# Two spectral layers on one Trainium2 core: the time transform taken ahead of the feature transform

## The chip, the cores and the metric

The kernel runs on one core of one Trainium2 chip. The time is that of the device in microseconds, from the start of the program to its end; lower is better. The engines are TensorE (PE, with its weight loads as PEld), VectorE (DVE), ScalarE (ACT), GpSimd (POOL) and SyncE (SP, which only issues DMAs).

## What is computed

The input x has 2048 time steps (rows) of 512 features. Two layers follow each other, each a spectral part and a feed-forward part:

```python
x = x + irfft2(rfft2(layernorm(x)) * (w_r + 1j * w_i))     # over time and features, 257 feature frequencies
n = layernorm(x)
x = x + ((n @ w_gate) * (n @ w_up)) @ w_down               # 512 -> 1792 -> 512
# both lines a second time, with the same weights
```

All is float32. The feed-forward part takes most of the time and is the same in both kernels; the change is in the spectral part.

## The kernel before, in words

**Layout.** The rows lie as 16 row tiles t of 128: time step 32p + 2t + jj stands on partition (jj, p), with p up to 63 and jj 0 or 1. `xs` holds x in SBUF all along.

**Spectral part, forward** (`fwd`, `fwd_rest`, L562 to L626), once per row tile: statistics of the layer norm and the reciprocal deviation (`stats`, `rstd`, tiles st, mv, rs); `fo`, sums and differences of the two halves of the features (additions on DVE, differences on POOL); `tp`, four turns of 128x128 on PE that bring the features to the partitions; `fb` and `fs`, a copy and a second fold of the features; `dp`, four 128x128 products with the cosine and sine matrices `df`, which end the feature transform; `us`, a copy that multiplies with the reciprocal deviation; `sp`, the part of the time transform that runs over p, with twiddles, as products over 64 partitions each (two at a time on the two halves of the array's rows) and 257 columns; copies of sp into `E`. Eight row tiles of layer 1 are turned through memory in place of tp (`by_memory`).

**Middle** (`middle`, L650 to L729), for 16 blocks of 16 feature frequencies: DVE turns 32x32 blocks of E into `T` (`turn`), `zp` multiplies with the 32-point transform `f2` over the 32 values of (t, jj), two ACT copies make `jz` (i times zp), DVE and POOL multiply with the filter (`wq`, `wr`), DVE adds into `ys` (in five blocks a second product with g2j adds on PE), `yp` transforms back, ACT copies into T, and DVE turns back into E. Frequency 256 goes apart (`tx`, `xp`, `hp`).

**Inverse** (`inv`, L731 to L778), per row tile: `vp`, the time part over p, four 128x128 products; a copy `vs`; `yi`, the inverse feature products (with 256 columns in "plain" tiles, 128 in "fold" tiles); additions of yi into xs; statistics for the next norm. vp of the first half of the frequencies waits for the first eight blocks only.

**Feed-forward part** (`unit`, `down` and others): products gx, gy, gw, gz, gv, db, ex to ev of three passes each. Six plain row tiles and two fold tiles of the inverse come before it or at its start; eight more tiles of the inverse lie inside its first half, and in layer 0 half of the next layer's `fwd` lies inside its second half.

**What sets the order.** The kernel's functions don't issue instructions; they record operations in a `Plan` (L175) with an engine, an estimated cost, the tiles read and written, and at some places a due time. `Plan.order` works the due times backwards, `run` lays the operations out by due time, and 250 moves from a list of seeds (`MOVES`) change due times again. Each engine then works its list strictly in order. All recorded operations are issued by one line of a helper, so nearly all rows of the profile say L417; tiles tell them apart. Buffers come in rings (`RINGS`): f (ten working tiles of 128x512), tw for the twiddles, and the eight PSUM banks x, y, w (one each), a (three), d (two).

The rates that the plan assumes for PE:

```python
pe(0.98, features, [(fs, 0), (fs, 1), df], [dp])             # forward, per row tile
pe(0.1 + 0.97 * (b - a) / 257, times, [u, tw], banks)         # sp
pe(0.86 * len(ms), unspec, [y, (q, 0), (q, 1)], [yp])         # middle, per block
pe(0.82 if fold else 1.73, features, [vs, di], [yi])          # inverse
```

## Time and profile before

| | |
|---|---|
| median of 3 runs | 1086.56 us |
| lowest and highest | 1084.35 and 1087.3 us |
| span of the profiled execution | 1082.8 us |
| granted TensorE clock | 1.000 |
| HBM read and written | 151.85 and 49.02 MB |

The profiled execution has no other time than its span, from the first to the last instruction; the runs' median lies 3.8 us above it. How to read it: the page gives busy times of the engines over the span; the views of the trace give the same by stretches of time (us, then busy us and number of instructions of PE, PEld, DVE, ACT, POOL, then the granted clock, the DMA share and GB/s), by groups of equal instructions, and as a timeline. A count in a row is of records: a product of plain float32 operands is two records, a turn or a product of the feed-forward part one.

### The profile page before, as it was taken

How to read it: one execution, taken by the hardware profiler on the slowest of the kernel's cores; microseconds unless marked ns; L12 is line 12 of the kernel's file. 1: busy time of each engine (PE TensorE's matmuls, PEld its weight loads, DVE VectorE, ACT ScalarE, POOL GpSimd, SP SyncE). 2: the span in 40 equal slices, each digit the busy share in tenths (PEclk: the TensorE clock that was granted, in tenths of full speed). 3: DMA queues.
4: the chain of work that ended last, by engine and by line, in shares of the span. 5: the costliest groups of instructions: out<-in, count | busy, mean ns of one | idle time of the engine just before them, and what ended most of it. 6: DMA issues, size and time to landing. Idle time of an engine off the chain costs nothing.

```text
span 1082.8 us, 18693 instructions
## 1 busy us (share of the span) xinstructions
PE 1062.9 (98%) x6404; PEld 913.4 (84%) x6404; DVE 839.6 (78%) x1660; ACT 445.7 (41%) x1021; POOL 766.5 (71%) x988
## 2 busy tenths in 40 slices
PE   8999999999999999999999999999999999999998
PEld 6748988888889988888997489888889998888887
DVE  8597877877868866676787978679897877667777
ACT  6777743443343223222346776124332521222330
POOL 7377798989999766658784627466597984676771
PEclk9999999999999999999999999999999999999999
DMA  7545357787771766575564313665877257546542
GB/s 270 219 156 195 117 202 252 232 273 226 255 262 51 235 233 202 158 226 181 144 205 160 125 61 104 204 198 165 222 251 211 70 199 248 173 167 198 192 145 78
DMA packets 104446, 202.08 MB, mean 187 GB/s; under 512 B 56352, under 2 KB 70176, under 8 KB 93344
## 3 DMA queue, kind: packets, MB, share of 16 engines
q0 software_dynamic: 16128, 102.77, 29.2%
q1 hardware_dynamic: 87936, 97.60, 27.6%
q8 instruction: 51, 0.84, 0.3%
q10 hardware_dynamic: 288, 0.52, 0.1%
q14 instruction: 43, 0.35, 0.1%
HBM read 151.85 MB, written 49.02 MB: 186 GB/s over the span
## 4 chain that ended last, share of the span: by engine, by line
PE 80%; POOL 6%; DVE 6%; ACT 2%; DMA 2%; issue 2%; SPq 0%; DVEq 0%; POOLq 0%; ACTq 0%
PE gz L417 13%; PE gx L417 12%; PE gv L417 7%; PE db L417 6%; PE gy L417 6%; PE gw L417 6%; PE ex L417 5%; PE ez L417 5%; PE yi L417 3%; PE ey L417 3%; PE sp L417 2%; PE ev L417 2%; PE ew L417 2%; PE dp L417 2%; PE vp L417 2%
## 5 line engine op out<-in xcount | busy, mean ns | idle before, releaser
L417 PE MATMUL gx<-xA,wt 128*128 128x512 f32 (+1 forms) x852 | 180.8, 347 | 2.9 <-ACT xA L417 1.1
L417 PEld LDWEIGHTS gx<-xA,wt 128*128 128x128 f32 x852 | 137.1, 189 | 21.3 <-DVE xA L417 1.4
L417 POOL TENSOR_TENSOR sf<-q,sf 128x256 fp32r<-128x256 f32 x101 | 75.1, 744 | 39.6 <-ACT sf L417 35.8
L417 DVE TENSOR_TENSOR xs<-xs,db 128x512 f32<-128x512 f32 x128 | 85.6, 683 | 14.8 <-PE db L417 14.5
L417 DVE TENSOR_TENSOR q<-gy,s 128x512 f32<-128x512 f32 (+1 forms) x71 | 41.0, 578 | 64.2 <-PE gy L417 46.5
L417 PE MATMUL gw<-xS,wt 128*128 128x512 f32 (+1 forms) x426 | 90.3, 347 | 0.3 <-POOL wt L417 0.3
L417 PE MATMUL gz<-xS,wt 128*128 128x512 f32 (+1 forms) x426 | 90.0, 347 | 0.1
L417 PE MATMUL gz<-xA,wt 128*128 128x512 f32 (+1 forms) x426 | 90.0, 347 | 0.0
L417 PE MATMUL gv<-xS,wt 128*128 128x512 f32 (+1 forms) x426 | 89.9, 346 | 0.0
L417 PE MATMUL gy<-xS,wt 128*128 128x512 f32 (+1 forms) x426 | 89.6, 346 | 0.0
L417 PE MATMUL db<-wd,h 128*128 128x512 f32 x336 | 89.1, 393 | 0.3
L417 ACT CAST sf<-q 128x256 fp32r<-128x256 f32 x101 | 41.1, 407 | 116.0 <-DVE q L417 71.8
L417 POOL TENSOR_TENSOR sf<-cc,sf 128x256 fp32r<-128x256 f32 x96 | 71.4, 745 | 19.1 <-ACT sf L417 18.7
L417 POOL DMA_DIRECT2D wt<-gu x72 | 40.5, 562 | 62.7 <-PE gz L417 42.9
L417 PEld LDWEIGHTS gz<-xA,wt 128*128 128x128 f32 x426 | 69.5, 189 | 10.1 <-DVE q L417 0.3
L417 PEld LDWEIGHTS gz<-xS,wt 128*128 128x128 f32 x426 | 68.6, 190 | 9.4 <-DVE q L417 0.7
L417 PEld LDWEIGHTS gw<-xS,wt 128*128 128x128 f32 x426 | 68.6, 190 | 9.0 <-POOL wt L417 0.5
L417 PEld LDWEIGHTS gv<-xS,wt 128*128 128x128 f32 x426 | 68.6, 190 | 8.9 <-issue 0.3
L417 PEld LDWEIGHTS gy<-xS,wt 128*128 128x128 f32 x426 | 68.5, 190 | 8.4
L417 ACT COPY s<-gx 128x512 f32<-128x512 f32 (+1 forms) x71 | 35.3, 496 | 87.6 <-PE gx L417 77.1
L417 PEld LDWEIGHTS db<-wd,h 128*128 128x128 f32 x336 | 60.7, 188 | 11.9 <-DVE xs L417 0.7
L417 POOL TENSOR_TENSOR wt<-rg,wt 128x512 fp32r<-128x512 f32 (+1 forms) x56 | 64.2, 1158 | 6.6 <-ACT wt L417 6.6
(171 smaller groups left out, 2644.2 us busy)
## 6 DMA issues: line engine op xcount, KB each, us to landing
wt<-gu POOLq DMA_DIRECT2D x36, 1024.0 KB, 5.5
wt<-gu POOLq DMA_DIRECT2D x36, 768.0 KB, 4.8
bf<-dn POOLq DMA_DIRECT2D x20, 1024.0 KB, 5.4
bf<-dn POOLq DMA_DIRECT2D x20, 768.0 KB, 4.7
gu<-wt SPq DMA_DIRECT2D x14, 1024.0 KB, 6.6
gu<-wt SPq DMA_DIRECT2D x14, 768.0 KB, 3.6
wq<-in_wf_dram SPq DMA_DIRECT2D x10, 1024.0 KB, 5.1
rg<-in_wb_dram SPq DMA_DIRECT2D x14, 512.0 KB, 5.0
```

Source lines behind the costliest of these rows:

```text
L417: ins = f(*args, **kw)
```

## The change

**Forward.** The time part over p comes first, straight on the rows: `tp` is now four products of fo (as stationary operand) with the twiddle matrix `tw`, 128 columns each. That brings the features to the partitions too, so the turns by PE and through memory, fb, us and sp go. The reciprocal deviation is multiplied into tw by ACT. Rows are real, so of 64 time residues 32 are kept; E holds features on the partitions, and 4 blocks, 16 row tiles, 16 pairs g and 8 values along the columns. In layer 0 the twiddles come in four loads.

**Middle.** 16 groups g, each a pair of time residues. Second feature fold `fs` (one half on POOL, one on DVE); `dp`, eight products with a stationary operand of 64 columns, whose results go to the lower and the upper 64 partitions in turn; a copy `zs`; `zp`, the 32-point transform; jz, filter and addition as before, always on DVE and POOL; `vq`, four 128x128 products that transform back and bring the frequencies to the partitions; a copy into E in runs of four elements. No 32x32 turns on E. Frequency 256 shares a column with frequency 0; a small DVE operation (8 columns) per filter load prepares that.

**Inverse.** yi first, straight from E, a copy or a fold into vs, then `yo`, one product of 512 columns, for the time part. yi needs all 16 groups.

**Filter.** Eight loads of 1 MB go to the buffers xA, xS and wd of the feed-forward part.

**rstd.** A pair of row tiles shares its small DVE operations (128x2 in place of two of 128x1).

**Order.** The moves are replaced by a list of due times, one for each operation (`DUES`). Rings: f 11 for 10, tw 8 for 4. The instructions of the feed-forward products keep their numbers; their order is another.

The core of the diff (constants, tables and the parts that follow from these are left out):

```diff
-    RINGS = {"x": 1, "y": 1, "w": 1, "a": 3, "d": 2, "f": 10, "tw": 4, "mv": 8, "rs": 8, "st": 2,
+    RINGS = {"x": 1, "y": 1, "w": 1, "a": 3, "d": 2, "f": 11, "tw": 8, "mv": 8, "rs": 8, "st": 2,
...
+        found = np.frombuffer(zlib.decompress(base64.b85decode("".join(DUES))), "<i2")
+        assert len(found) == len(ops)
+        for o, due in zip(ops, found):
+            o["due"] = int(due) * 0.1
+        return self.run()
...
-        ts = V.tensor_scalar
-        for i in range(n):
-            c = lambda j, i=i: v()[:, j, i:i + 1]
-            m = lambda j, i=i: mv()[:, i, j:j + 1]
-            dve(10, lambda c=c, m=m: ts(c(1), m(1), EPS, c(1), op0=ALU.add, op1=ALU.mult), [(mv, i)], [(v, 1, i)])
-            dve(10, lambda c=c: ts(c(2), c(1), -1.5, c(0), op0=ALU.add, op1=ALU.mult), [(v, 0), (v, 1, i)], [(v, 2, i)])
-            if not fwd:
-                dve(10, lambda c=c, m=m: ts(c(3), m(0), -1.0, c(2), op0=ALU.mult, op1=ALU.mult), [(v, 2, i), (mv, i)],
-                    [(v, 3, i)])
+        c = lambda j: v()[:, j, :n]
+        m = lambda j: mv()[:, :n, j]
+        vs = lambda j: [(v, j, i) for i in range(n)]
+        dve(10, lambda: stt(c(1), m(1), EPS, c(1), op0=ALU.add, op1=ALU.mult), mvs, vs(1))
+        dve(10, lambda: stt(c(2), c(1), -1.5, c(0), op0=ALU.add, op1=ALU.mult), [(v, 0), *vs(1)], vs(2))
+        if not fwd:
+            dve(10, lambda: stt(c(3), m(0), -1.0, c(2), op0=ALU.mult, op1=ALU.mult), [*vs(2), *mvs], vs(3))
...
-        tw = twiddle(tf, t)
+        tw = tws[t] if tws else twiddle(tf, t)
+        act(128, lambda: A.mul(tw(), tw(), nm.v()[:, 2, i:i + 1]), [(nm.v, 2, i)], [tw], more=0.1)
         fo = temp("fo", "f", (128, 4, 128))
         x0, x1 = (xs[:, t, 256 * h:256 * h + 256].rearrange("p (a d) -> p a d", a=2) for h in range(2))
         pool(256, lambda: gtt(fo()[:, 2:4], x0, x1, ALU.subtract), [("xs", t)], [(fo, 1)])
-        dve(256, lambda: tt(fo()[:, 0:2], x0, x1, ALU.add), [("xs", t)], [(fo, 0)], two=True)
-        fs, fb = temp("fs", "f", (128, 4, 128)), temp("fb", "f", (128, 4, 128))
-        if mem:
-            by_memory(lambda: fo().rearrange("p a d -> p (a d)"), f"f{t}", lambda: fb().rearrange("p a d -> p (a d)"), [fb],
-                      None, [(fo, 0), (fo, 1)])
+        if on_pool:
+            pool(256, lambda: gtt(fo()[:, 0:2], x0, x1, ALU.add), [("xs", t)], [(fo, 0)])
         else:
-            tp = bank("tp", tags(t)[0])
-
-            def turn():
-                for j in range(4):
-                    TE.transpose(tp()[:, 128 * j:128 * j + 128], fo()[:, j], ident)
-
-            pe(0.44, turn, [(fo, 0), (fo, 1), "ident"], [tp])
-        quarter = lambda v, j: v().rearrange("p (a j) d -> p a j d", j=2)[:, :, j]
-        ta, tb = (lambda j=j: tp().rearrange("p (a j d) -> p a j d", a=2, j=2)[:, :, j] for j in range(2))
-        if mem:
-            pool(256, lambda: gtt(fs()[:, 2:4], quarter(fb, 0), quarter(fb, 1), ALU.subtract), [fb], [(fs, 1)])
-            pool(256, lambda: gtt(fs()[:, 0:2], quarter(fb, 0), quarter(fb, 1), ALU.add), [fb], [(fs, 0)])
-        elif on_pool:
-            act(512, lambda: A.copy(fb(), tp().rearrange("p (j d) -> p j d", j=4)), [tp], [fb])
-            pool(256, lambda: gtt(fs()[:, 2:4], quarter(fb, 0), quarter(fb, 1), ALU.subtract), [fb], [(fs, 1)])
-        else:
-            act(256, lambda: A.copy(quarter(fb, 1), tb()), [tp], [fb])
-            dve(256, lambda: tt(fs()[:, 2:4], ta(), quarter(fb, 1), ALU.subtract), [tp, fb], [(fs, 1)])
-        if not mem:
-            dve(256, lambda: tt(fs()[:, 0:2], ta(), quarter(fb, 1), ALU.add), [tp, fb], [(fs, 0)])
-        dp = bank("dp", tags(t)[1])
+            dve(256, lambda: tt(fo()[:, 0:2], x0, x1, ALU.add), [("xs", t)], [(fo, 0)], two=True)
+        tp = bank("tp", tag(t))
+
+        def spread():
+            for b in range(4):
+                TE.matmul(tp()[:, 128 * b:128 * b + 128], fo()[:, b], tw(), start=True, stop=True, skip_group_check=True)
+
+        pe(0.9, spread, [(fo, 0), (fo, 1), tw], [tp])
+        act(512, lambda: A.copy(E()[:, :, t].rearrange("p b g e -> p b (g e)"), tp().rearrange("p (b c) -> p b c", b=4)), [tp], [(E, t)], due=due)
...
+        def load(self, n):
+            load(1024, lambda: SP.dma_start(self.part(n), wf[:, n]), (), [self.key[n]], ahead=FAHEAD)
+            dve(8, lambda: stt(self.part(n)[:, :, :, 0], self.part(n)[:, :, :, 0], 0.5, hp[:, :, 4 * n:4 * n + 4],
+                               op0=ALU.mult, op1=ALU.add), ["hp"], [self.key[n]])
...
-            pe(0.1 + 0.97 * (b - a) / 257, times, [u, tw], banks)
...
-            pe(0.86, lambda z=z, n=n: TE.matmul(z(), f2, T()[:, 16 * n:16 * n + 16], start=True, stop=True), [(T, n), "midt"], [zp])
...
+        fs = temp("fs", "f", (128, 4, 16, 8))
+        folds = FOLDS[g % len(FOLDS)]
+        for i, op in ((0, ALU.add), (1, ALU.subtract)):
+            args = [*es], [(fs, i), (E, "g", g, i)]
+            if folds[i] == "P":
+                pool(256, lambda i=i, op=op: gtt(fs()[:, 2 * i:2 * i + 2], src(0), src(1), op), *args)
+            else:
+                dve(256, lambda i=i, op=op: tt(fs()[:, 2 * i:2 * i + 2], src(0), src(1), op), *args, two=True)
+        dp = bank("dp", "xy"[g % 2] if g < 13 else "x")
...
+            f4 = fs().rearrange("p j t (e q) -> p j (t e) q", q=2)
+            for q in range(2):
+                for j, c, odd in ((0, 0, 0), (2, 1, 0), (3, 0, 1), (1, 1, 1)):
+                    o = 256 * q + 128 * odd
+                    TE.matmul(dp()[64 * c:64 * c + 64, o:o + 128], f4[:, j, :, q], df()[:, j], start=True, stop=True,
+                              skip_group_check=True)
...
+        zs = temp("zs", "f")
+        act(512, lambda: A.copy(zs(), dp()), [dp], [zs])
+        zp = bank("zp", "da"[g % 2])
+
+        def across():
+            if g:
+                TE.matmul(zp(), f2, zs(), start=True, stop=True)
             else:
+                for q, m in enumerate((f20, f2)):
+                    TE.matmul(zp()[:, 256 * q:256 * q + 256], m, zs()[:, 256 * q:256 * q + 256], start=True, stop=True, skip_group_check=True)
+
+        pe(0.86, across, [zs, "midt"], [zp])
+        jz, y = temp("jz", "f"), temp("ys", "f")
+        act(512, lambda: A.mul(jz()[0:64], zp()[64:128], -1.0), [zp], [(jz, 0)], more=0.11)
+        act(512, lambda: A.copy(jz()[64:128], zp()[0:64]), [zp], [(jz, 1)], more=0.11)
+        w = W.key[g // 2]
+        dve(512, lambda: tt(zp(), zp(), W(g, 0), ALU.mult), [(jz, 0), (jz, 1), w], [zp])
+        pool(512, lambda: gtt(jz(), jz(), W(g, 1), ALU.mult), [w], [(jz, 0), (jz, 1)])
+        dve(512, lambda: tt(y(), zp(), jz(), ALU.add), [zp, (jz, 0), (jz, 1)], [y])
+        vq = bank("vq", "w" if g < 13 else "yw"[g % 2])
+
+        def back():
+            for q in range(2):
+                for par in range(2):
+                    o = 256 * q + 128 * par
+                    TE.matmul(vq()[:, o:o + 128], y()[:, o:o + 128], g2 if g or q else g20, start=True, stop=True, skip_group_check=True)
+
+        pe(0.92, back, [y, "midt"], [vq])
+        into = lambda: E()[:, :, :, g].rearrange("p b t (q e) -> p q (b t) e", q=2)
+        act(512, lambda: A.copy(into(), vq().rearrange("p (q c e) -> p q c e", q=2, e=4)), [vq], [(E, "g", g, 0), (E, "g", g, 1)], due=due)
...
-            pe(0.46, lambda par=par: times(par), [tw, *((E, "b", n) for n in range(8 * par, 8 * par + 8))], [(vp, par)], due=early)
...
-        act(512, lambda: A.copy(vs(), vp()), vps, [vs])
...
+                TE.matmul(yi()[:, o], E()[:, i, t], di()[:, i, 0:128 if fold else 256],
...
+        pe(0.9 if fold else 1.73, features, [*((E, "g", g, 0) for g in range(16)), di], [yi], due=early)
...
+            act(512, lambda: A.copy(vs(), yi()), [yi], [(vs, 0), (vs, 1)])
...
+        pe(0.88, lambda: TE.matmul(yo(), tw(), vs(), start=True, stop=True), [tw, (vs, 0), (vs, 1)], [yo])
```

More of the change, by code (lines that the diff above doesn't have):

```diff
@@ new lines, in consts @@
+    f[0, 1] = g[0, 1] = (1.0 - 2.0 * (p % 2))[:, None]
+    tf = np.zeros((2, 64, 16, 16, 2, 2, 2))
+    ti = np.zeros((64, 2, 16, 2, 64))
+    for jj in range(2):
+        tf[jj, :, :, :, :, jj] = f.reshape(16, 2, 2, 64, 16, 2)[..., jj].transpose(3, 4, 0, 2, 1)
+        ti[:, jj, :, jj] = g.reshape(64, 64, 16, 2)[..., jj].transpose(0, 2, 1)
+    w = np.exp(-2j * np.pi * (np.outer(j, j) % 32) / 32)
+    late = np.exp(-1j * np.pi * j / 32)[:, None] * w
+    unit = np.array([1.0, 1j])
+    fs, gs = [], []
@@ L311, in run @@
         for o in ops:
-            if not o["n"] and not o["out"]:
+            if not o["n"]:
                 enter(o)
@@ L346, in run @@
             first = min(a for a, _ in nexts)
-            if first > mark + 20.0:
-                mark = first
-                marks.append((len(out), first, {g: list(q) for g, q in rings.items()}, dict(free), bus, port, dict(after)))
             at, o = min((c for c in nexts if c[0] <= first + look), key=lambda c: (c[1]["due"], c[1]["i"]))
-            if o["e"] == "PE":
-                assert not pace or at < pace[done]
-                done += 1
             ready[o["e"]].remove(o)
@@ L1178 @@
             begins.append(t)
[L1179 to L1181 removed]
+            u = UNITS[layer][k >= 18]
+            t += (UFIRST if k < 2 else u[0]) if half is not None else u[1] if k < 12 else u[2]
             if k == 1:
```

489 lines of the change are left out of this document (196 added, 293 removed), and 35 rows, old and new, of the table MOVES.

## The prediction

> **What bounds the kernel now.** I read the page first, then busy time by stretches, then TensorE's timeline at the stage borders, then the groups of instructions. (In all rows: PE is TensorE, PEld its weight loads; a timeline row is start, duration, instructions; a group row ends in busy time, mean ns of one, and idle time before.)
>
> ```profile
> span 1082.8 us, 18693 instructions
> PE 1062.9 (98%) x6404; PEld 913.4 (84%) x6404; DVE 839.6 (78%) x1660; ACT 445.7 (41%) x1021; POOL 766.5 (71%) x988
> ```
> ```profile
> 70.00:80.00 10.00, 10.00 (x28) 4.74 (x27) 10.00 (x18) 8.64 (x16) 9.64 (x10) 1.00 0.20 60
> 700.00:800.00 100.00, 100.00 (x598) 88.91 (x598) 86.43 (x164) 34.56 (x79) 64.71 (x94) 1.00 0.67 201
> ```
> PE is busy 98% of the span and all of 700 to 800 us, a stretch of the feed-forward part. So PE work that is saved inside that part is saved time, and a new order of it can hardly win more. In the middle of a spectral stage (70 to 80) PE and DVE are both full, and POOL nearly. The spectral stages stand between these rows:
>
> ```profile
> 49.21 1.98 PE L417 MATMUL zp<-T,midt 128*128 128x512 f32 x4 [0.63 <-DVE T L417]
> 85.96 1.70 PE L417 MATMUL vp<-tw,E 128*128 128x128 f32 x12 [1.01 <-DVE E L417]
> 109.22 0.86 PE L417 MATMUL gx<-xA,wt 128*128 128x256 f32 x5 [0.34 <-DVE xA L417]
> ...
> 588.60 4.56 PE L417 MATMUL zp<-T,midt 128*128 128x512 f32 x10 [0.63 <-DVE T L417]
> 623.88 1.70 PE L417 MATMUL vp<-tw,E 128*128 128x128 f32 x12 [1.01 <-DVE E L417]
> ```
> The forward part of layer 0 ends at 49.2; the middles last 36.8 us (49.21 to 85.96) and 35.3 us (588.60 to 623.88); the feed-forward part begins near 109.
>
> **What one piece of PE work costs.** A record's duration holds its drain, so I use distances from start to start.
>
> ```profile
> 30.65 0.60 PE L417 MATMUL tp<-ident,fo 128*128 128x128 f32 x4
> 31.08 1.06 PE L417 MATMUL dp<-df,fs 128*128 128x128 f32 x8
> ...
> 37.69 2.00 PE L417 MATMUL sp<-us,tw 64*128 64x257 f32 x16
> 39.62 0.55 PE L417 MATMUL tp<-ident,fo 128*128 128x128 f32 x3
> ```
> ```profile
> 582.00 2.94 PE L417 MATMUL dp<-df,fs 128*128 128x128 f32 x24
> 584.87 3.10 PE L417 MATMUL sp<-us,tw 64*128 64x257 f32 x32
> ```
> ```profile
> 615.29 1.02 PE L417 MATMUL zp<-T,midt 128*128 128x512 f32 x2
> 616.14 1.02 PE L417 MATMUL yp<-ys,midt 128*128 128x512 f32 x2
> ```
> ```profile
> 97.25 1.10 PE L417 MATMUL vp<-tw,E 128*128 128x128 f32 x8
> 98.19 1.06 PE L417 MATMUL yi<-di,vs 128*128 128x128 f32 x8
> ```
> Four turns tp: 0.43 us. Four 128x128 products (dp): 2.87/3 = 0.957. One row tile's time transform sp: 1.93/2 = 0.965. One 512-column product: 0.855. One vp: 0.94.
>
> **Layer 0, forward.** PE's work per row tile falls from tp + dp + sp to one spread tp of four 128x128 products: 0.957 (same shape as dp). PE is then no longer the limit; DVE is, which has statistics, additions and the small rs operations to do.
>
> ```profile
> 4.48 0.69 DVE L417 BATCH_NORM_STATS2 st<-xs 128x6 f32<-128x512 f32 x1 [3.60 <-DMA xs<-in_x_dram]
> ...
> 31.59 0.21 DVE L417 TENSOR_SCALAR rs<-rs 128x1 f32<-128x1 f32 x1
> ```
> ```profile
> L417 DVE TENSOR_TENSOR fs<-tp,fb 128x256 f32<-128x256 f32 x24 | 10.0, 416 | 6.2 <-ACT fb L417 4.8 <-POOL cc L417 1.3
> L417 DVE TENSOR_SCALAR rs<-mv,rs 128x1 f32<-128x1 f32 x96 | 17.8, 206 | 2.7 <-ACT rs L417 2.1
> L417 ACT COPY T<-yp 128x512 f32<-128x512 f32 x32 | 18.8, 587 | 10.3 <-PE yp L417 9.9
> L417 POOL TENSOR_TENSOR fs<-fb 128x256 f32<-128x256 f32 x40 | 29.4, 743 | 16.7 <-ACT fb L417 16.2 <-POOL fs L417 0.3
> ```
> DVE's list runs without a break from 4.5 to 31.8. It loses sixteen fs (6.7 us) and twelve of 32 rs (2.5: pairs of tiles share one) and gains two on hp (0.4): it ends at 23.2. Then, for the last two tiles: scaling of two twiddles on ACT (128 columns, not in the trace; between rs of 0.21 and a copy of 512 of 0.59, I take 0.3 each, 0.6), two spreads 1.9, the copy into E 0.6, a fold of E on POOL 0.74, five hand-overs of 0.2 (row below): 28. If DVE wins nothing, 36.7; better than 26 I do not see. **Gain 49.2 - 28 = 21.2.**
>
> ```profile
> 48.61 0.56 ACT L417 COPY E<-sp 128x193 f32<-128x193 f32 x2 [0.20 <-PE sp L417]
> ```
>
> **The middles** get dearer on PE. Before, a layer had 16 zp, 16 yp and five more yp of 0.855: 31.6 us. After, each of 16 groups has dp, zp and vq. vq is four 128x128 products, 0.957; zp 0.855. dp is new in form: eight products that fill 64 of the array's columns each, in pairs on the two column halves. No row shows column halves. From below: four products' worth, less the last weight load, 0.85; from above: eight one after the other, 8 x 0.957/4 = 1.91. The nearest rows are sp, which does the same with halves of the rows: 0.965 for four products of some 256 columns, where one after the other would be 2 x 0.855 = 1.71. So pairs ran together there, 0.11 over a perfect 0.855. I take 0.957 and 0.14 for the two changes of form per group: 1.1. Group: 1.1 + 0.855 + 0.957 = 2.91; 16 groups 46.6; first group's wait 1, drain of the last 1.5, copy of the last group into E and hand-over 0.8: 49.9. This part had one cover that goes: vp could start on half the frequencies, yi needs all 16 groups.
>
> The others must hold 2.91 per group:
>
> ```profile
> L417 ACT ACTIVATE jz<-zp 64x512 f32<-64x512 f32 x22 | 12.9, 594 | 3.5 <-PE zp L417 3.3
> L417 POOL TENSOR_TENSOR jz<-jz,wr 128x512 f32<-128x512 f32 x16 | 20.2, 1274 | 9.3 <-ACT jz L417 9.3
> L417 ACT COPY E<-sp 128x257 f32<-128x257 f32 x60 | 20.2, 394 | 12.9 <-PE sp L417 12.7
> L417 DVE TENSOR_TENSOR ys<-zp,jz 128x512 f32<-128x512 f32 x22 | 14.7, 666 | 0.0
> L417 DVE STREAM_TRANSPOSE T<-E 128x512 f32<-128x512 f32 x32 | 20.9, 684 | 11.3 <-ACT E L417 11.3
> ```
> ACT: two copies of 0.587, two jz of 0.594: 2.36. POOL: fold 0.743 and jz 1.274: 2.02, and in layer 0 the feed-forward weights' forms stand between them. DVE: fold 0.42, two of 0.67: 1.8; its two transposes of 0.69 per block, which filled it, go. None is over 2.91, but each works in order: behind a late jz on POOL stand the next fold and the weight forms, behind a late copy on ACT the next zs. For that I take 2 us per middle (from 0 to rival 2's pace). **Loss: 49.9 + 2 - 36.8 = 15.1 and 49.9 + 2 - 35.3 = 16.6.**
>
> The inverse neither gains nor loses: yo (0.855) takes the place of vp (0.94), 1.4 us less per layer; 1.4 us of vp that was done inside each middle is lost.
>
> **Layer 1, forward**, half of it inside the feed-forward part. PE before: 16 x (0.957 + 0.965) + 8 x 0.43 = 34.2; after 16 x 0.957 = 15.3; 18.9 less. The end of it is a chain:
>
> ```profile
> 575.08 0.69 DVE L417 TENSOR_TENSOR xs<-xs,ez 128x512 f32<-128x512 f32 x1
> ```
> ```profile
> L417 ACT ACTIVATE rs<-mv,eps 128x2 f32<-128x2 f32 x30 | 8.9, 297 | 10.1 <-DVE mv L417 9.9
> L417 ACT ACTIVATE rs<-rs 128x2 f32<-128x2 f32 x30 | 6.2, 205 | 0.5
> ```
> The last addition ends at 575.8, the first zp comes 12.8 later, and PE is at work all through. After, from that addition: two statistics 1.4, rs on ACT 0.5 and DVE 0.4, twiddles 0.6, two spreads 1.9, copy 0.6, fold 0.74, seven hand-overs 1.4: 7.5. In the new order five spreads (4.8) stand there: 2.7 idle, 2.1 more than the 0.63 in the row of 588.60. **Gain 16.8.** SP's queue: all eight 1 MB filter loads now wait for buffers of the feed-forward part.
>
> ```profile
> wq<-in_wf_dram SPq DMA_DIRECT2D x10, 1024.0 KB, 5.1
> ```
> 5.1 us from issue to landing; the last product that reads these buffers comes before the last additions, so the first is there in time, and each serves two groups (5.8 us).
>
> **Sum.** 21.2 - 15.1 + 16.8 - 16.6 = 6.3 us less: 1082.8 becomes 1076.5. The median of the runs is 3.8 over the profiled span: **1080.3, say 1080**.
>
> **Rivals.**
> 1. *Column halves do not run together* (slower). Then dp is 1.91 and 32 groups cost 32 x 0.81 = 26 us more: 1106. It decides from dp = 1.1 + 6.3/32 = 1.30. For it: no row shows the form. Against it: sp.
>
> ```profile
> L417 PE MATMUL dp<-df,fs 128*128 128x128 f32 x256 | 33.8, 279 | 2.7 <-DVE fs L417 1.6 <-POOL fs L417 1.1
> L417 PEld LDWEIGHTS dp<-df,fs 128*128 128x128 f32 x256 | 30.6, 191 | 6.2 <-DVE fs L417 2.5 <-issue 2.0 <-POOL fs L417 1.3
> ```
> A milder form: the halves' weight loads (30.6/256 = 0.12 each, 0.06 for half the columns, sixteen of them) do not lie beside products: 0.85 + 0.96 = 1.81, 1103. Those rows speak against it: loads of 30.6 and products of 33.8 lay beside each other with all rows of the array in use. The Trainium skill, page "TensorE: Matmul & The Clock Gate", Part 3 (packing small matmuls), has it that a weight load overlaps running matmuls only where the row groups differ; column halves share theirs. By that rule rival 1 would hold; the trace does not agree with it for dp.
>
> 2. *The middles are paced by ACT* (slower). If the copy into E, in runs of four elements, takes twice its 0.587, and three of ACT's four steps per group wait a hand-over of 0.2 for PE, the pace is 2.36 + 0.59 + 0.6 = 3.55 in place of 2.91: 16 x 0.64 - 2 = 8.2 per middle, 1096. For it: ACT is at 81% of the pace already. Against: no row shows a copy slowed by its pattern (E<-sp, with steps of two, took 394 ns for 257).
>
> 3. *The forward part does not shrink as far*: half of what DVE loses returns as waits for ACT's twiddles, first dp at 32.5: 1085, no change.
> 4. *Better*: dp 0.9 and no stalls: 6.4 + 4 less, 1070.
>
> That the change does not do what it says is excluded by the built programs' instruction lists: sp, vp, yp and all 32x32 turns on E are gone, and the feed-forward products have the same number.
>
> **How the numbers follow.** About 0.3% (3.3 us) is what a measurement can tell. Forecast 0.45 (0.39 faster, 0.06 same, by its own 4 us of scatter), rival 1 0.14 (slower), rival 2 0.15 (slower), rival 3 0.12 (0.04 faster, 0.08 same), rival 4 0.14 (faster). Faster 0.57, same 0.14, slower 0.29. The range goes from 1068, 2 us under rival 4, to 1098, which takes in rival 2 and a dp of up to 1.67, and leaves out the full price of rival 1.
>
> **What would show it.** First dp at 28 us and about 7.5 after the last addition of layer 0; dp with its next start 1.1 apart; middles of 50 to 52 us with PE nearly full; no sp. The forecast falls if dp is over 1.3, if PE waits for ACT or POOL inside the middles, or if the feed-forward part between them is no longer full.

## The result, and the profile after

The changed kernel is not faster: its median is **1089.68 us** (10 runs, 1085.10 to 1096.35), that of the kernel before, run beside it, 1084.82 us (10 runs, 1083.40 to 1087.35). The ratio is **1.0051, with a 95% interval of 1.0027 to 1.0074**: 5.5 us slower by the ratio (4.9 by the medians), where 6.3 less was forecast. The 3.8 us that the forecast put between span and median came from three runs; ten lie 2.0 above the span of 1082.8, so differences and spans are compared below. The profiled execution is the slowest of the ten (1096.35, span 1094.6), so its stages are read for their places and causes, and sizes are taken from the kernel of the experiment `rs_one_source`, whose runs lie closer together.

The page of the changed kernel, span and busy times, and its row of SP's filter loads (count, KB each, us from issue to landing):

```profile
span 1094.6 us, 18695 instructions
...
PE 1050.0 (96%) x6528; PEld 906.3 (83%) x6528; DVE 827.9 (76%) x1530; ACT 432.1 (39%) x979; POOL 763.4 (70%) x976
...
wq<-in_wf_dram SPq DMA_DIRECT2D x16, 1024.0 KB, 10.3
```

The change does what it says: PE has 12.9 us less to do (1062.9 to 1050.0). But the span grew by 11.8, so PE's idle time grew from 19.9 to 44.6 us. The work was saved; the idle time has to be found. TensorE's timeline of the changed kernel at the borders of the stages:

```profile
32.91 2.55 PE L394 MATMUL dp<-df,fs 128*64 128x128 f32 x32 [1.20 <-DVE fs L394]
...
41.12 1.97 PE L394 MATMUL dp<-df,fs 128*64 128x128 f32 x32
43.02 1.16 PE L394 MATMUL vq<-midt,ys 128*128 128x128 f32 x8
...
82.64 1.56 PE L394 MATMUL yi<-di,E 128*128 128x256 f32 x6 [0.67 <-ACT E L394]
...
108.69 0.88 PE L394 MATMUL gx<-xA,wt 128*128 128x256 f32 x6
...
578.96 2.54 PE L394 MATMUL dp<-df,fs 128*64 128x128 f32 x32 [1.14 <-DVE fs L394]
...
629.47 1.78 PE L394 MATMUL yi<-di,E 128*128 128x256 f32 x7 [0.67 <-ACT E L394]
...
656.21 0.28 PE L394 MATMUL gx<-xA,wt 128*128 128x256 f32 x1
```

The 32 records of two dp (sixteen each) and the next start lie 1.90 apart (41.12 to 43.02), so one dp takes 0.95. Of the kernel before, two rows of the same view are needed beside those shown, the first product of each feed-forward part:

```profile
108.50 0.39 PE L417 MATMUL gx<-xA,wt 128*128 128x256 f32 x1 [1.13 <-ACT xA L417]
...
647.17 0.38 PE L417 MATMUL gx<-xA,wt 128*128 128x256 f32 x1
```

The starts of these rows, subtracted, give the stages. The last two columns are kernels of the experiments, read in the same way:

| stage, us | before | forecast | after | rs_one_source | wq_by_need |
|---|---|---|---|---|---|
| to the first dp (before: zp), layer 0 | 49.21 | 28 | 32.91 | 31.63 | 33.73 |
| middle, layer 0, to the first vp or yi of the inverse | 36.75 | 51.9 | 49.73 | 51.20 | 49.74 |
| inverse, layer 0, to the first gx | 22.54 | 22.5 | 26.05 | 26.56 | 26.56 |
| feed-forward part and layer 1's forward | 480.10 | 463.3 | 470.27 | 461.68 | 459.57 |
| middle, layer 1 | 35.28 | 51.9 | 50.51 | 50.51 | 50.52 |
| inverse, layer 1 | 23.29 | 23.3 | 26.74 | 27.02 | 27.01 |
| the rest | 435.63 | 435.6 | 438.39 | 435.50 | 434.67 |
| span | 1082.8 | 1076.5 | 1094.6 | 1084.1 | 1081.8 |

The middles came out within 2.2 us of the forecast. The largest miss is 7.0 us in the feed-forward part and layer 1's forward, which had been taken as full. Between 110 and 545 us PE is idle for 8.7 us, in the kernel before for 3.1. The changed kernel's timeline around the longest such wait, DVE first, then POOL, then PE:

```profile
331.74 4.62 DVE L394 SCALAR_TENSOR_TENSOR rs<-mv,rs 128x2 f32<-128x2 f32 x1
336.28 0.68 DVE L394 TENSOR_TENSOR xs<-xs,db 128x512 f32<-128x512 f32 x1
...
331.07 0.74 POOL L394 TENSOR_TENSOR rw<-rw 128x256 f32<-128x256 f32 x1
331.77 0.74 POOL L394 TENSOR_TENSOR h<-q,h 128x256 fp32r<-128x256 f32 x1
332.46 1.43 POOL L394 TENSOR_TENSOR xf<-xf 128x256 f32<-128x256 f32 x2
333.85 1.81 POOL L394 TENSOR_TENSOR xA<-xf,xA 128x768 fp32r<-128x768 f32 x1
335.62 0.72 POOL L394 TENSOR_TENSOR u<-rw,u 128x256 fp32r<-128x256 f32 x1
...
338.06 0.98 PE L394 MATMUL gz<-xA,wt 128*128 128x256 f32 x6 [3.65 <-DVE c L394]
```

An rs operation on two columns takes 4.62 us. It starts while POOL works through rw, and it ends at 336.36; POOL's u, the last of a run of operations without a break, ends at 336.34. Behind it on DVE stand xs and then c, which TensorE's gz needs: 3.65 us idle. So this is no wait for a semaphore (the row has no "idle before"): the instruction itself is long.

### The profile page after: what moved, and what is told of

It is laid out like the page before. It is cut to its first block, busy times and chain, and to the rows that moved or that the text cites. A ratio compares the mean times of both kernels' runs of the same rounds, so it can differ in the third digit from the quotient of the medians.

```text
span 1094.6 us, 18695 instructions
## 1 busy us (share of the span) xinstructions
PE 1050.0 (96%) x6528; PEld 906.3 (83%) x6528; DVE 827.9 (76%) x1530; ACT 432.1 (39%) x979; POOL 763.4 (70%) x976
## 4 chain that ended last, share of the span: by engine, by line
PE 71%; DVE 8%; POOL 8%; issue 4%; DMA 4%; ACT 4%; SPq 0%; POOLq 0%; ACTq 0%; DVEq 0%
PE gz L394 11%; PE gx L394 11%; PE gy L394 6%; PE gw L394 6%; PE gv L394 6%; PE ex L394 5%; PE ez L394 5%; PE db L394 4%; PE dp L394 3%; PE zp L394 3%; PE ey L394 2%; PE ew L394 2%; PE ev L394 2%; POOL wt L394 2%; DVE xs L394 2%
## 5 line engine op out<-in xcount | busy, mean ns | idle before, releaser
L394 POOL TENSOR_TENSOR sf<-cc,sf 128x256 fp32r<-128x256 f32 x103 | 75.8, 739 | 33.4 <-ACT sf L394 32.6
L394 PE MATMUL db<-wd,h 128*128 128x512 f32 x336 | 93.0, 403 | 0.6 <-DVE xs L394 0.3
L394 POOL TENSOR_TENSOR sf<-q,sf 128x256 fp32r<-128x256 f32 x89 | 65.5, 737 | 39.2 <-ACT sf L394 38.9
L394 PE MATMUL gy<-xS,wt 128*128 128x512 f32 (+1 forms) x426 | 91.9, 352 | 0.3 <-DVE q L394 0.3
L394 ACT CAST sf<-cc 128x256 fp32r<-128x256 f32 x103 | 41.8, 406 | 89.3 <-PE ex L394 32.9
L394 ACT CAST sf<-q 128x256 fp32r<-128x256 f32 x89 | 36.1, 406 | 100.3 <-PE ez L394 32.3
## 6 DMA issues: line engine op xcount, KB each, us to landing
wq<-in_wf_dram SPq DMA_DIRECT2D x16, 1024.0 KB, 10.3
```

The costliest lines, as they stand in the source:

```text
L394: ins = f(*args, **kw)
```

## The theories

**Port theory.** Before, an rs operation was a tensor_scalar: one column from SBUF, and the other values as scalars of each partition. To do two columns in one instruction the change made it a scalar_tensor_tensor, which reads two SBUF operands. Such an instruction waits while POOL works, the other form doesn't. The Trainium skill says this of the hardware (page "SBUF — State Buffer", sections "SBUF: two separate sides" and "Who interferes with whom"): a VectorE instruction with two SBUF inputs takes its second through a read interface shared with GpSimd and contends with a GpSimd instruction that reads SBUF; the lock is exclusive and held for a whole instruction, and the other is blocked meanwhile. With at most one SBUF input, outside VectorE's 2-port modes, there is no such conflict. The rows agree in kind, but by holding for one instruction this rs would have gone ahead at 331.81, where rw ends, and it waited for five more.

**Rivals.** (a) The clock: the changed kernel's mean granted clock was 0.992, before 1.000; a slow early stretch could cost all of it. (b) The order: due times were searched for durations that the chip doesn't keep, so waits fall anywhere. (c) Full price of parts that I costed at nothing: the inverse, and the second feed-forward part.

## The experiments

All ratios are to the kernel before, run in the same set.

| kernel | median us (runs) | ratio, 95% interval |
|---|---|---|
| again | 1093.09 (9) | 1.0059, 1.0034 to 1.0083 |
| rs_one_source | 1086.17 (12) | 1.0006, 0.9993 to 1.0019 |
| before_rs_two_source | 1096.69 (5) | 1.0101, 1.0081 to 1.0122 |
| warm6 | 1091.64 (12) | 1.0054, 1.0034 to 1.0075 |
| fo_pool_yo | 1086.96 (12) | 1.0019, 1.0005 to 1.0033 |
| fo_pool_yo_warm | 1087.32 (11) | 1.0021, 1.0008 to 1.0035 |
| wq_late | 1085.72 (12) | 1.0015, 1.0002 to 1.0028 |
| wq_late_dve | 1084.90 (11) | 1.0000, 0.9991 to 1.0010 |
| wq_by_need | 1082.22 (6) | 0.9972, 0.9958 to 0.9987 |
| filled | 1082.75 (11) | 0.9983, 0.9971 to 0.9994 |
| wq_by_need2 | 1082.95 (12) | 0.9983, 0.9969 to 0.9997 |

### again: the changed kernel, unchanged

> The changed kernel once more, nothing edited, as the base of this set (its first profile fell on the slowest of ten runs, 1096.35 us against a median of 1089.68). Port theory (small rs operations of DVE with two SBUF operands wait until a run of POOL work ends): such waits come by chance of timing, so the sum of rs times above their usual 0.16 us is large here too (10 us or more), with at least one of over 1 us in front of a TensorE stall, but at other places than 331.7 us. Rival (the order itself has fixed holes): the same stalls at the same places, 3.65 us near 334 among them. Time 1085 to 1096.

1.0059 confirms the first ratio. The long rs operation stands at the same place in its timeline:

```profile
331.87 4.30 DVE L394 SCALAR_TENSOR_TENSOR rs<-mv,rs 128x2 f32<-128x2 f32 x1
```

Where I had looked for the waits to move from run to run, in these two profiles they don't: seven of the eight rs operations over 1 us stand in the same places, so the fixed order has a large part in where DVE meets POOL. The clock speaks against rival (a), as far as it means an early stretch: in this profile it was 1.00 all through layer 0's forward part, and the first dp still came late, at 33.10.

### rs_one_source: the rs operations as before, one operand and one column each

```diff
-        dve(10, lambda: stt(c(1), m(1), EPS, c(1), op0=ALU.add, op1=ALU.mult), mvs, vs(1))
+        dve(10, lambda: each(lambda i: ts(c(1, i), m(1, i), EPS, c(1, i), op0=ALU.add, op1=ALU.mult)), mvs, vs(1))
```

and the two lines behind it alike; the order of everything else stays.

> In the changed kernel each small rs operation is written as before the change: tensor_scalar with one column at a time, so two instructions of about 0.21 us for a pair in place of one two-operand instruction of 128x2. Lists, order and due times stay. Port theory: no rs record over 0.3 us, the rs total falls from about 32 us to about 20, the TensorE stalls behind rs (334, 354, 225, 776 us in the first profile) go; 3 to 7 us faster than the changed kernel, so 1083 to 1087, and a narrower scatter. Rival (order): the stalls stay under other names and the time stays within 2 us of the changed kernel.

1.0006: the loss is gone, though DVE now has 160 rs operations in place of 84. The feed-forward part and layer 1's forward shrink from 470.27 to 461.68. The stretch from 110 to 545 us of the changed kernel, by windows (us, busy us and count of PE, PEld, DVE, ACT, POOL, clock, DMA share, GB/s):

```profile
110.00:545.00 435.00, 426.31 (x2425) 370.04 (x2424) 335.93 (x587) 150.47 (x335) 341.16 (x415) 1.00 0.59 195
```

and of rs_one_source:

```profile
110.00:545.00 435.00, 433.63 (x2499) 377.79 (x2498) 333.15 (x627) 152.96 (x339) 343.94 (x420) 1.00 0.59 197
```

PE's idle time there goes from 8.7 to 1.4 us. The clock of 1.00 is a rounded mean: in the changed kernel it was 0.50 from 339.3 to 342.7, right behind the wait of 3.65 us, which can cost 1.7 us more (half of 3.4). `again` and warm6 have the same behind that wait (from 338.5 and 336.2), rs_one_source has no such window in this stretch. So a share of the loss comes by way of the clock, but behind the wait.

### before_rs_two_source: the kernel before with two-operand rs operations

```diff
-            dve(10, lambda c=c, m=m: ts(c(1), m(1), EPS, c(1), op0=ALU.add, op1=ALU.mult), [(mv, i)], [(v, 1, i)])
+            dve(10, lambda c=c, m=m: stt(c(1), m(1), EPS, c(1), op0=ALU.add, op1=ALU.mult), [(mv, i)], [(v, 1, i)])
```

and the other two alike: same number, same columns, same order, another form.

> The kernel before with one thing from the change: its rs operations (one column each, their number and order unchanged) as scalar_tensor_tensor with both tensor operands in SBUF, in place of tensor_scalar. Port theory: rs records that were never over 0.22 us now reach 0.6 to several us, 10 to 25 us in sum above 0.16, and some of them end in front of a TensorE stall: 2 to 6 us slower than before. Rival (the form of the small operations doesn't matter, only the order and the structure): rs at 0.15 to 0.2 us throughout, time within 1 us of before.

1.0101: the form alone makes the kernel before 11 us slower, more than the 2 to 6 expected, and at a clock of 1.00 in every stretch of its profile. The shortest, median and longest rs operation (ns; then first and last start) of this kernel, by the view of one tile:

```profile
L417 DVE SCALAR_TENSOR_TENSOR rs<-mv,rs x96: 120/159/4211, 6.3 to 821.5; 128x1 f32<-128x1 f32 x96
```

of the kernel before:

```profile
L417 DVE TENSOR_SCALAR rs<-mv,rs x96: 178/205/216, 6.5 to 809.1; 128x1 f32<-128x1 f32 x96
```

of the changed kernel:

```profile
L394 DVE SCALAR_TENSOR_TENSOR rs<-mv,rs x50: 122/160/4622, 9.2 to 830.1; 128x2 f32<-128x2 f32 x46, 128x1 f32<-128x1 f32 x4
```

and of rs_one_source:

```profile
L394 DVE TENSOR_SCALAR rs<-mv,rs x96: 173/204/214, 9.0 to 820.3; 128x1 f32<-128x1 f32 x96
```

The two-operand form is the shorter one by its median, 0.16 against 0.21 us (the changed kernel's 34 other rs operations: 161 ns, at most 1573). Its tail is what costs: 4.2 and 4.6 us at worst, where the other form never leaves 0.17 to 0.22. A price taken from a median can't show that. In this kernel too the longest lies beside POOL at work:

```profile
346.99 3.65 POOL L417 TENSOR_TENSOR xA<-xf,xA 128x768 fp32r<-128x768 f32 x2
350.57 0.75 POOL L417 TENSOR_TENSOR xf<-xf 128x256 f32<-128x256 f32 x1
...
347.12 4.28 DVE L417 SCALAR_TENSOR_TENSOR rs<-mv,rs 128x1 f32<-128x1 f32 x2
...
352.25 0.96 PE L417 MATMUL db<-wd,h 128*128 128x512 f32 x3 [2.40 <-DVE xs L417]
```

The pair of rs ends at 351.40, POOL's run at 351.32, and PE waits 2.40. The long waits aren't the usual ones. In the changed kernel, 111 us earlier (DVE, then POOL):

```profile
220.98 1.21 DVE L394 SCALAR_TENSOR_TENSOR rs<-rs 128x2 f32<-128x2 f32 x1
222.22 1.21 DVE L394 SCALAR_TENSOR_TENSOR rs<-mv,rs 128x2 f32<-128x2 f32 x1
...
220.88 1.29 POOL L394 TENSOR_TENSOR wd<-rw,wd 128x512 fp32r<-128x512 f32 x1 [1.44 <-DVE xs L394]
222.13 1.29 POOL L394 TENSOR_TENSOR h<-q,h 128x512 fp32r<-128x512 f32 x1
```

Each rs ends with the one POOL operation beside it, and POOL goes straight on (its next starts at 223.37). Read over the whole trace: of the 84 rs operations 50 start with no POOL operation under way, and none of these takes over 0.17 us. The other 34 start beside one, and none ends ahead of it: 30 end with it or at most 0.1 us later, three with the operation behind it, and the one at 331.74 with the sixth. In rs_one_source, 56 of the 80 rs operations that start beside a POOL operation end while it is still at work. So mostly the wait is for one instruction, as the Trainium skill's page has it; what lets POOL pass several times isn't shown.

This settles the port theory for nearly the whole of the loss: the two-operand form alone costs one kernel 11 us, and undoing it, together with the pairs of columns, wins 5.7 in the other.

### warm6: six products on zeros at the start

```diff
+        for n in range(6):
+            TE.matmul(wp(), warm()[:, 0:128], warm(), start=True, stop=True)
```

> In the changed kernel six more products of 512 columns on zeros follow the warming products at the start, to fill TensorE's idle 5.18 us ahead of the first tp (results unused). Clock theory: the granted clock of 0.50 between 8 and 15 us goes to 1.0, the first 24 tp take 2.9 us in place of 5.04, and the first dp comes 1 to 2 us earlier than 32.9. Rival (ScalarE's copies and twiddles pace the forward part of layer 0): the tp get faster, but the later tp wait longer for ScalarE and the first dp stays at 32.5 to 33; no difference in time.

1.0054, as without them. The clock was held at 1.00 from 8 to 15 us and fell later instead; its window from 15 to 24:

```profile
15.00:24.00 9.00, 6.66 (x41) 6.31 (x41) 9.00 (x28) 5.49 (x17) 4.66 (x6) 0.81 1.04 414
```

The first dp stood at 33.13. So six early products move the dip, and no gain shows.

### fo_pool_yo: other two-operand operations out of POOL's way

This kernel and those behind it start from rs_one_source. What that left at the border to layer 1, in its timeline: one of the additions fo beside POOL (DVE, POOL, PE):

```profile
555.02 2.29 DVE L394 TENSOR_TENSOR fo<-xs 128x256 f32<-128x256 f32 x1
...
554.93 0.74 POOL L394 TENSOR_TENSOR sf<-q,sf 128x256 fp32r<-128x256 f32 x1
555.62 1.41 POOL L394 TENSOR_TENSOR fo<-xs 128x256 f32<-128x256 f32 x2
...
558.90 1.37 PE L394 MATMUL ez<-bf,sf 128*128 128x256 f32 x5 [2.01 <-DVE wq L394]
...
801.52 0.95 PE L394 MATMUL ez<-bf,sf 128*128 128x256 f32 x6 [1.93 <-DVE xs L394]
```

The last row is a second loss: ahead of it DVE stands for 3.14 us, up to 798.30, until a yo on PE, and PE then waits 1.93 for what comes behind on DVE. The edit moves fo additions to POOL (layer 0: tiles 8 to 15; layer 1: tile 12) and one yo ahead of an ev product:

```diff
+            add = gtt if t in (range(8, 16) if tws else (12,)) else tt
-            dve(256, lambda: tt(fo()[:, 0:2], x0, x1, ALU.add), [("xs", t)], [(fo, 0)], two=True)
+            dve(256, lambda: add(fo()[:, 0:2], x0, x1, ALU.add), [("xs", t)], [(fo, 0)], two=True)
...
+    yo = done.pop(where(3303))
+    done.insert(where(3706), yo)
```

> The kernel with one-operand rs, and three stalls relieved in place, each read in its own stage (no other operation moves). (a) Layer 0: eight of the sixteen additions fo go from DVE to POOL. If DVE's list paces the forward part there (27.7 us of it in place of the 18.7 that the prediction had), the first dp comes 2 to 3 us earlier than 31.6; if ScalarE or the landing of x paces it, it stays at 31 or later. (b) Layer 1: the one addition fo that took 2.29 us at 555.0 beside 2.8 us of POOL work (two operands in SBUF, as the rs had) goes to POOL. Port theory: the 2.0 us of TensorE idle at 556.9 goes and the first dp of layer 1 comes 1.5 to 2 us earlier still; rival: the ez product waits as long for something else. (c) Second feed-forward part: one yo is issued before the ev product in place of two products later. If the transpose of DVE that starts at yo's end holds up the additions behind it, the 1.93 us idle at 799.6 falls under 0.5; rival: the transpose waits for something else and the idle stays. All three: 4 to 6 us less than 1086.2, so 1080 to 1082; if only (b) or none hold, 1084 to 1086.

1.0019, no gain. The 1.93 fell to 0.39, but from layer 1's gx to the end it took 435.75 in place of 435.50: no net gain from the yo. Layer 0's first dp came at 34.89, but in a stretch with a clock of 0.64 (12 to 24 us), so that one kernel couldn't tell the edit from the dip.

### fo_pool_yo_warm: the same, with five early products

> The same with five more products on zeros at the start, so that TensorE is never idle over 1 us ahead of the first tp. Where the granted clock fell to 0.5 near the start of the forward part (one stretch of 3.4 us in the profile of the one-operand kernel costs 1.7 us of TensorE), that goes; but in the run of the unchanged kernel the clock stayed at 1.0 there with the same first dp. Clock theory: 1 to 2 us less than without. Rival (DVE or ScalarE paces this stage): within 1 us of it.

1.0021. With a clock of 1.00 there, the first dp came at 31.17, against 31.63 in rs_one_source: half a microsecond for eight additions taken off DVE. At the border to layer 1 the wait that left fo went to the next two-operand operation, wq, a fix of eight columns (DVE, POOL, PE):

```profile
556.38 2.46 DVE L394 SCALAR_TENSOR_TENSOR wq<-wq,hp 128x8 f32<-128x8 f32 x1
...
556.03 2.78 POOL L394 TENSOR_TENSOR fo<-xs 128x256 f32<-128x256 f32 x4
...
560.16 1.16 PE L394 MATMUL tp<-tw,fo 128*128 128x128 f32 x8 [2.61 <-ACT tw L394]
```

wq starts 0.35 after POOL's run of fo and ends with it, at 558.84 against 558.81. The distance from layer 0's first gx to layer 1's first dp stays: 461.68 before the edit, 461.25 after it.

### wq_late and wq_late_dve: wq behind the last rs

wq_late is fo_pool_yo_warm with two of the wq operations moved:

```diff
+    for i in (2693, 2687):
+        fix = done.pop(where(i))
+        done.insert(where(2681), fix)
```

> The kernel with one-operand rs, the additions fo on POOL, the earlier yo and the warming products, and one step more: in layer 1 two of the small wq operations (two operands in SBUF, 128x8) stand behind DVE's last rs operation in place of between the last additions of the feed-forward part. In the profile without this step the stall had only changed its carrier: wq took 2.46 us at 556.4 beside 2.8 us of POOL work, and tp then waited 2.61 us. Port theory: with no two-operand operation left there no DVE record of this stretch is over 0.9 us, the tp wait of 2.61 falls under 0.8, and the first dp of layer 1 comes 1.5 to 2.5 us earlier after the start of the feed-forward part (461.3 us there). Rival (another chain, over the landing of the loads or ScalarE, ends as late): the wait moves once more and the distance stays within 0.5 us of 461.3.

1.0015; the distance is 461.15, so this wins nothing either. The second kernel also puts layer 0's fo additions back on DVE (`add = gtt if t == 12 and not tws else tt`):

> The same, but with the eight additions fo of layer 0 back on DVE. If DVE's list paces the forward part of layer 0, the first dp comes 1.5 us or more later than with them on POOL (31.2); if TensorE does (first tp at 10, then 15.3 us of tp and about 3 us of waits in the first half), it stays within 0.7 us of it. Time within 1.5 us of the other kernel of this set; the better of the two 1083 to 1086.

1.0000, first dp at 31.71 with fo on DVE and 31.77 with half of it on POOL: in these two profiles DVE's fo don't set the end of layer 0's forward part. At the border to layer 1 DVE's list now stands on the filter loads themselves (wq_late_dve, DVE and PE):

```profile
565.81 0.17 DVE L394 SCALAR_TENSOR_TENSOR wq<-wq,hp 128x8 f32<-128x8 f32 x1 [1.12 <-DMA wq<-in_wf_dram]
568.37 0.55 DVE L394 SCALAR_TENSOR_TENSOR wq<-wq,hp 128x8 f32<-128x8 f32 x1 [2.39 <-DMA wq<-in_wf_dram]
...
569.30 0.88 PE L394 MATMUL dp<-df,fs 128*64 128x128 f32 x12 [2.51 <-DVE fs L394]
```

The loads of parts 3 to 6 serve groups 6 to 13, yet their wq hold up the fs of the first group, because DVE works in order. This is a new wait of the change that I hadn't counted: I followed the loads only to the moment when the filter is needed, not to the first operation on them.

### wq_by_need: four wq operations issued where their groups need them

```diff
-    for i in (2693, 2687):
+    for i in (2687, 2689, 2691, 2693):
         fix = done.pop(where(i))
-        done.insert(where(2681), fix)
+        done.insert(where(2728), fix)
```

Operation 2728 is the third zp of layer 1's middle.

> The last kernel (additions of layer 0 on DVE) with four of layer 1's eight small wq operations, for the filter parts 3 to 6 that groups 6 to 13 use, issued behind the first groups of the middle in place of ahead of them. In the profile without this step the last one ahead of the first fs stood 2.4 us on the landing of its filter load, and with it the whole list of DVE. Load theory: the first dp of layer 1 then waits 1.1 to 1.3 us in place of 2.51 and comes 1.2 to 1.5 us earlier after the start of the feed-forward part (461.3 us); the middle keeps its 49.9 us; the time falls by the same, to 1083 to 1084. Rival: in the middle the four operations wait for their loads or for POOL in front of the zp products, the middle grows by 1 us or more, and nothing is won.

0.9972: faster than the kernel before. The first dp of layer 1 waits 1.14 in place of 2.51:

```profile
569.12 1.29 DVE L394 TENSOR_TENSOR fs<-E 128x256 f32<-128x256 f32 x2 [2.92 <-ACT E L394]
```

DVE now stands ready for 2.92 us before fs; no wq is in its way. The distance falls from 461.29 to 459.57; the middle behind it grows from 49.94 to 50.52, so 1.1 of the 1.7 us are left.

### filled and wq_by_need2: is the clock in layer 0 worth anything

`filled` puts eleven products on constants where PE waits in layer 0's forward part:

```diff
+            for n in range({3: 4, 4: 7}.get(t, 0) if tws else 0):
+                TE.matmul(tp()[:, 0:128], ident, ident, start=True, stop=True, skip_group_check=True)
```

> The best kernel so far (small wq operations by need) with TensorE's two longest waits in the forward part of layer 0 filled: four products of 128 columns on constants ahead of the fourth tp and seven ahead of the fifth, written to the bank that the tp overwrites. Clock theory: the granted clock of 0.50 that stood between 20 and 24 us (and in other runs at other places before 26) goes, the twelve tp behind the fifth take 11.5 us in place of 13.6, the first dp comes near 31.5 in place of 33.7, the runs lie closer together and their median 1 us lower. Rival (the clock falls wherever it likes, or DVE and ScalarE pace this stage): the first dp stays between 31 and 34 from run to run and the median within 0.5 us.

`wq_by_need2` is wq_by_need again, in the same set:

> The kernel with the small wq operations by need once more, unchanged, on the chip and in the rounds of the filled one: its median again 1081.5 to 1083.5, its ratio to before under 1.

1082.75 and 1082.95: the same. `filled` had a clock of 1.00 from 8 us up to its last microsecond, and its first dp still came at 33.82, that of `wq_by_need2` at 31.86 and that of wq_by_need, the same kernel, at 33.73. Rival (a), a slow early stretch, falls with that: a dip may lengthen a single run (the first dp at 34.89, above, where the clock was 0.64), but the products that were to keep the clock up move no median. What moves the first dp by 2 us between runs stays open. And wq_by_need holds: 0.9983, with an interval below 1.

## Why the prediction was wrong, step by step

**The rs operations: the step that failed.** The forecast has "twelve of 32 rs (2.5: pairs of tiles share one)" as a gain. It priced their number and took the duration of the old form; the new form, which reads two SBUF operands, and its 84 uses, from layer 0's forward part on to 830 us, were not priced. It cost 1.0059 - 1.0006 = 0.53%, **5.7 us** (the two intervals leave about 3 to 9). The forecast's last sign of being wrong, the feed-forward part no longer full, is what came. On DVE the waits sum to more: the groups of rs operations of the changed kernel (count, busy, mean ns),

```profile
L394 DVE SCALAR_TENSOR_TENSOR rs<-mv,rs 128x2 f32<-128x2 f32 (+1 forms) x50 | 19.5, 392 | 3.1 <-ACT rs L394 2.5
L394 DVE SCALAR_TENSOR_TENSOR rs<-rs 128x2 f32<-128x2 f32 (+1 forms) x34 | 12.5, 369 | 0.7
```

hold 50 x (392 - 160) + 34 x (369 - 161) ns = 18.7 us over their medians, so about a third of it reached the end. Without it the kernel stands at 1086.17, 0.7 us above the kernel before where 6.3 less was forecast. So with the old form the forecast would still have been missed. The other 7.0 us (7.6 in the spans of rs_one_source against the forecast), term by term:

**Layer 0's forward part, 3.6 us too short** (31.63 against 28). The forecast ended DVE's list at 23.2 (its terms, 31.8 - 6.7 - 2.5 + 0.4, give 23.0). The last rs of rs_one_source is

```profile
27.64 0.33 DVE L394 TENSOR_SCALAR rs<-rs 128x1 f32<-128x1 f32 x2
```

which ends at 27.97, 4.8 later; the tail from there to dp is 3.7 in place of 4.8. DVE's groups in the kernel before, from 0 to 31.85, show why (busy, mean ns):

```profile
L417 DVE TENSOR_TENSOR fs<-tp,fb 128x256 f32<-128x256 f32 x10 | 4.1, 408 | 0.0
```

"It loses sixteen fs (6.7 us)": only ten of them lay in that stretch, 4.1 us. The rs operations that remain take 5.4 us in place of 6.3 (0.9 gained, not 2.5), and fo takes 1.6 less. That is 6.6 lost where 9.2 was counted: 2.6 of the 4.8. Of the other 2.2, DVE stands idle for 1.3: 0.69 until a row tile has landed and 0.63 until an rs on ACT; 0.9 isn't taken apart. In size this is near rival 3 (first dp at 32.5, 1085), but that rival's mechanism, waits for ACT's twiddles, isn't what these numbers show.

**The inverse, 4.1 and 3.7 us too short.** "The inverse neither gains nor loses" held for the work per tile, but not for its place. Groups of yi in the kernel before, from 85.9 to 108.4:

```profile
L417 PE MATMUL yi<-di,vs 128*128 128x256 f32 (+1 forms) x64 | 13.1, 353 | 0.0
```

and in rs_one_source, from 82.8 to 109.3 and, the second row, from 621.5 to 648.5:

```profile
L394 PE MATMUL yi<-di,E 128*128 128x256 f32 (+1 forms) x80 | 15.0, 341 | 2.5 <-DVE xs L394 1.8 <-ACT E L394 0.7
...
L394 PE MATMUL yi<-di,E 128*128 128x256 f32 (+1 forms) x88 | 16.1, 335 | 1.7 <-DVE mv L394 0.8 <-ACT E L394 0.7 <-DVE xs L394 0.2
```

Sixteen and 24 records more: two and three fold tiles of eight records, 0.957 each, which the new order does before the feed-forward part, 1.9 and 2.9 us. They are moved, not added. The rest, 2.2 and 0.8, is about PE's idle time in front of yi (2.5 and 1.7 in these rows, of which 0.7 each stand ahead of the stage), which the kernel before hadn't in layer 0.

**The feed-forward parts, "a new order of it can hardly win more".** I read this as: nothing can be lost there either. Layer 0's and layer 1's forward together came out 1.6 us under the forecast, which is what the two moved tiles are worth (1.9). In layer 1 three tiles are moved ahead and should shorten the rest by 2.9; it stayed (435.50 against 435.6). The kernel before from 800 to 1060 us:

```profile
800.00:1060.00 260.00, 260.00 (x1668) 236.98 (x1667) 195.02 (x327) 78.58 (x182) 190.28 (x263) 1.00 0.55 178
```

and rs_one_source:

```profile
800.00:1060.00 260.00, 256.83 (x1655) 233.49 (x1656) 195.37 (x331) 78.69 (x184) 195.36 (x269) 1.00 0.56 184
```

3.2 us of waits took what the moved tiles had won. fo_pool_yo took most of one of 1.93 away there, and the stretch grew no shorter. That the whole of these small waits comes from the new due times (rival b) is argued, not shown: no kernel put the old order's places back.

**The filter loads, "the first is there in time".** The first was; later ones were waited for by DVE's wq ahead of time, 1.12 and 2.39 us. From issue to landing a load took 10.3 us, not 5.1. Issuing wq by need was worth 1.7 us of the distance to layer 1's first dp, of which the middle gave 0.6 back.

**The middles were right in sum**, 51.20 and 50.51 against 51.9, in part by luck. A dp with results on the two column halves takes 0.95 in the rows above, below the 1.1 that I took, which is 2.4 us less per middle; the middles came out only 0.7 and 1.4 shorter, so starts, drains and waits took 1.0 to 1.7 more than the 5.3 that I gave them. Rival 1, 1.91 for each, is refuted. The Trainium skill's rule that I weighed there (page "TensorE: Matmul & The Clock Gate", Part 3: loads overlap running matmuls only across row groups) would give 1.81 or more; the trace doesn't agree with it. Rival 2, ACT's pace of 3.55 per group and 60 us per middle, didn't come.

The sum of the terms, rs_one_source against the forecast: 3.6 - 0.7 + 4.1 - 1.6 - 1.4 + 3.7 - 0.1 = 7.6 us, the difference of the spans (1084.1 and 1076.5). The last version, wq_by_need, has the change's spectral stages, the old form of rs, five early products, one fo on POOL, the earlier yo, and the wq operations at their place. From its page (span 1081.8):

```profile
PE 1050.1 (97%) x6538; PEld 904.9 (84%) x6538; DVE 817.1 (76%) x1605; ACT 433.3 (40%) x979; POOL 764.5 (71%) x977
```

PE has 12.8 us less to do than in the kernel before; 0.17 to 0.28% of the time, 1.8 to 3.0 us, comes out of it.

**Open.** The ten runs of the changed kernel spread over 11.3 us, those of the kernel before over 4.0; rs_one_source's over 4.7. The two profiles of the changed kernel were of long runs and show the same waits; what a run of 1085 us does otherwise wasn't seen. The clock goes with it: the four runs over 1092 us have a mean of 0.989 to 0.994, the three shortest 0.997 or 0.998, and 0.005 of 1090 us is 5.5 us. Whether the clock makes these runs long or waits make both isn't shown.

## What to carry to other kernels

When instructions are merged, price the new form and not only the smaller number: count the SBUF operands of each small VectorE operation, and look whether GpSimd works beside it. Read the longest instruction of a group beside its mean; a median of 0.16 with a maximum of 4.6 is a wait inside the instruction, which no "idle before" shows; compare its end with the ends of GpSimd's operations. And a stretch that is full before a change is full by its order: a new order must earn that again, so cost it at some waits, not at nothing.

## What the hardware showed that I had not expected

- A two-operand VectorE operation of 128x2 values takes 0.16 us where POOL stands idle, and beside a POOL operation it ends no sooner than that (the two exceptions, in before_rs_two_source, stand beside a POOL instruction of 0.57 us that issues a DMA): all 20 rs operations over 0.5 us in the changed kernel's profile, and all 33 in that of before_rs_two_source, end 0.01 to 0.03 us behind the end of one.
- Mostly that is the operation under way (30 of 34), but it can be passed by more: 4.62 us over six operations, 4.28 for a pair of rs with three, 2.46 over four.
- The wait can go to the next two-operand operation when the first is taken away (fo 2.29, then wq 2.46); here removing the first won 0.4 us of 461.68.
- The longest wait stood at the same place in two executions, 4.62 and 4.30 us at 331.74 and 331.87, though the kernel's time varies by 11 us.
- TensorE's granted clock fell to 0.50 in windows of 3.4 or 6.8 us, in layer 0's forward part at other places from run to run (0.64 from 12 to 24 us in one profile, 0.81 from 15 to 24 in another, 1.00 in a third). Nine profiles have 20 such windows ahead of their end, and in the 3.4 us ahead of each TensorE was busy for less than half the time (0 to 47%).
